# Attention scores in plain float32, two heads side by side, in a fused attention and two-layer-expert kernel

## Chip, cores and metric

One core of one Trainium2 chip. The time is device microseconds from start to end of one execution of the whole kernel; less is better. Engines: PE (TensorE matmul; PEld is its weight load), DVE (VectorE), ACT (ScalarE), POOL (GpSimd), SP (issues DMAs).

## What is computed

The reference is rotary attention, a gated layer (`x @ w_in`, times its sigmoid, `@ w_out`), and four relu experts weighted by `domain_probs`. The change touches the attention alone:

```python
batch, n_heads, seq, head_dim = (2, 8, 576, 64)
q_rot, k_rot = rotate(q), rotate(k)     # x1*cos - x2*sin, x1*sin + x2*cos
scores = q_rot @ k_rot.T / 8
attn = exp(scores - max(scores))
attn = attn / (sum(attn) + 1e-09)
out = attn @ v
```

All inputs and the output are float32.

## The kernel before

**Pairs and units.** The 16 heads are worked in 8 pairs of heads. Head 0 of a pair lies in partitions 0 to 63 of the tiles `xk` and `xq` (64 rows for the 64 head dimensions), head 1 in partitions 64 to 127. A pair has nine units: a unit (hf, r, h) is 128 query rows of head h against all 576 keys; r runs from 0 to 3, and the ninth unit (r = 4, h = 2) holds the last 64 query rows of both heads. Units 0 to 3 make half 0 of the pair, units 4 to 8 half 1.

**What a unit goes through.** `scores` (S below) multiplies query and key into a score tile `s` of two PSUM banks, 288 keys in each. `rowmax` (M, DVE) takes the negative row maximum. `expo` (E, ACT) makes the exponentials and their sums. `transp` (T, PE) transposes 4 x 128 columns into a PSUM bank `b`; `high` (H) copies that bank to SBUF on ACT, or, for the units listed in `EVD`, `low` (L) does it on DVE. The columns 512 to 575 of four units are transposed together into a further bank ("five" in the code, `p5`). `av` multiplies the transposed exponentials by the values in a bank, for half 1 of the pair before (`L0`, `L1`) and half 0 of this one (`P0`, `P1`); its result is copied to `xu` by ACT. `norm` (`Ln`, `Pn`) spreads the reciprocal sums into a bank by PE, and DVE multiplies `xu` by it (line 492), after which ACT and POOL split the product in two parts for the next layer.

**Keys and queries before.** Rotary is three operations for the key (k1 to k3) and three for the query (q1 to q3), on POOL or DVE (lines 252 to 259). The float32 key and query are then split in a high and a low float32r part: `key_high` on ACT, `key_low` on DVE, `query_high` and `query_low` on POOL (k4, k5, q4, q5), and `spread` sends six DMAs on SP's queue, so that a unit's stationary operand holds the high part of the query in 64 rows and the low part in the other 64, and the moving operand the keys twice. A unit's scores are four float32r matmuls of 128 rows and 288 columns (line 324), and ten matmuls for the ninth unit (lines 329 to 335). The first four units of the first pair alone go by `first_scores` (line 350): plain float32, 64 rows, one head, straight from `xq` and `xk`.

**PSUM.** Eight banks: two score tiles of two banks (`psS`), and four banks of the pool `ps1`, which the transposes, `p5`, `av` and `norm` take in turn.

**What sets the order.** The order of the instructions is written out by hand and kept (`manual_schedule`). Each unit is one step s = 0 to 8 of its pair, and the step's string in `ORDER` (`ORDER0` for the first pair, `ORDER2` for the last two) gives the order of atoms: S is the scores of unit i+2, M its row maximum, E the exponentials of unit i+1, T, H and L the transposes and copies of unit i, B the entries of `PLAN` (`av` and `norm`), v and V the copy and the multiply behind them, X the split, W and w the widening of the next layer's weights (`WIDE`). `OFF`, `OFF1`, `OFF2` place loads and rotary in half steps against the pair's start. Each engine works its own instructions strictly in this order.

**Behind the attention** come the gated layer and the experts, which nothing of the change touches; their first matmuls stand at the end of the last pair.

Of the kernel before, what the change touches and what calls it, by code (L numbers as in the profile page):

```python
# [38 lines left out]
NWARM = 13
NCST = 2 * 576 + 128 + 64 + 128  # L40
# [7 lines left out]
def fused_kernel(ctx, tc, q, k, v, w_in, w_out, dprobs, w1, w2, cst, out):  # L48
    nc = tc.nc
# [18 lines left out]
    mask = cs[:, 1344:1472]  # L68
    xh2 = pers.tile([128, 4, NT], F32R, name="xh")
# [145 lines left out]
    for p in range(NPAIR):  # L215
# [15 lines left out]
        if p == 0:  # L231
            P.units = [P.units[j] for j in FIRST]
# [28 lines left out]

    def parts(P, nm):
        t = kkp.tile([128, 2, 576], F32R, name=nm + "2")
        setattr(P, nm + "2", t)

    def key_high(P):
        for h in range(2):
            rows = (TOP, LOW)[h]
            nc.scalar.activation(KK[P.i][rows, 0, 576 * h:576 * h + 576], P.xk[rows, 0, :], AF.Copy,
                                 scale=0.125 if P.n > 1 else 1.0)  # L270

    def key_low(P):
        for h in range(2):
            rows = (TOP, LOW)[h]
            hi, lo = (KK[P.i][rows, z, 576 * h:576 * h + 576] for z in range(2))
            nc.vector.scalar_tensor_tensor(lo, P.xk[rows, 0, :], 0.125 if P.n > 1 else 1.0, f32(hi),
                                           ALU.mult, ALU.subtract)

    def spread(P):
        for h in range(2):  # L280
            k_ = f32(KK[P.i][:, :, 576 * h:576 * h + 576])
            nc.sync.dma_start(k_[(LOW, TOP)[h]], k_[(TOP, LOW)[h]])
            for z in range(2):
                nc.sync.dma_start(f32(QQ[P.i][64 * z:64 * z + 64, 640 * h:640 * h + 576]),
                                  f32(P.q2[64 * h:64 * h + 64, z, :]))
            made.add((P, "spread", h))

    def query_high(P, g, rows=ALL, cols=FULL):
        if g is nc.scalar:
            g.copy(P.q2[rows, 0, cols], P.xq[rows, 0, cols])  # L290
        else:
            g.tensor_scalar(P.q2[rows, 0, cols], P.xq[rows, 0, cols], 1.0, 1.0, ALU.mult, ALU.mult)

    def query_low(P, g, rows=ALL, cols=FULL):
        g.tensor_tensor(P.q2[rows, 1, cols], P.xq[rows, 0, cols], f32(P.q2)[rows, 0, cols], ALU.subtract)
# [4 lines left out]
    def prep_small(P):  # L300
# [4 lines left out]
        P.s = {}  # L305
# [4 lines left out]
    def scores(P, un):  # L310
        hf, r, h = un
        if P.n < 2 and P.units.index(un) < (NUN, NUN1)[P.n]:
            return first_scores(P, un)
        for h_ in (0, 1) if h == 2 else (h,):
            assert (P, "spread", h_) in made
        s = psS.tile([128, 2, 512], F32, name="s")
        kk, qq = KK[P.i], QQ[P.i]
        if r < 4:
            c0 = 704 if h else 0
            lq = qq[:, c0 + 128 * r:c0 + 128 * r + 128]  # L320
            for a in range(2):
                for nb in range(2):
                    c = 576 * h + 288 * nb
                    nc.tensor.matmul(s[:, nb, 0:288], lq, kk[:, a, c:c + 288],  # L324
                                     start=(a == 0), stop=(a == 1))
        else:
            for a in range(2):
                for nb in range(2):
                    nc.tensor.matmul(s[:, nb, 0:288], qq[:, 512:640], kk[:, a, 288 * nb:288 * nb + 288],
                                     start=(a == 0), stop=False)  # L330
            lq = qq[:, 576:704]
            for a in range(2):
                nc.tensor.matmul(s[:, 0, 0:288], lq, kk[:, a, 640:928], start=False, stop=(a == 1))
# [907 lines left out]
```

## Time and profile before

| | |
|---|---|
| median of 3 runs | 748.18 us (748.15 to 749.2) |
| the profiled execution's own time | 749.54 us |
| span of its records, first to last instruction | 746.8 us |
| PE busy by the records | 735.7 us (99%) |
| DVE, ACT, POOL busy | 484.8, 301.5, 267.1 us |
| mean granted TensorE clock | 0.988 |

The profiled execution lies 1.4 us above the median, and 2.7 us of its time lie outside its span. Matmul records overlap (a record lasts from the issue of its first column to the end of its results), so a busy PE says little by itself; what a matmul costs is read from the distance between the starts of neighbouring records. A plain float32 matmul leaves two records, a float32r matmul or a transpose one. PEclk 1.00 is 2.4 GHz, 0.50 is 1.2 GHz. The mark `[0.23 <-PE b L298]` behind a row says that the engine stood idle for 0.23 us and which instruction ended that.

### The profile page before, as it was taken

What the parts mean: (1) busy time and instruction counts of PE and PEld (TensorE: products, weight loads), DVE (VectorE), ACT (ScalarE), POOL (GpSimd) and SP (SyncE); (2) the same over time, 40 slices, a digit from 0 to 9 for tenths busy, and PEclk for the clock granted to TensorE, in tenths of its full rate; (3) what the DMA queues carried; (4) which work ended last, traced back from release to release, by engine and by line L of the source; (5) the groups of instructions that cost most, each with busy time, mean ns of one, the idle gap of its engine ahead of it and who ended that gap; (6) DMA issues with size and microseconds to landing.
All of it is one profiled execution on the core that took longest, in us unless ns stands there. A gap on an engine that the chain in (4) does not pass through costs nothing.

```text
span 746.8 us, 11306 instructions
## 1 busy us (share of the span) xinstructions
PE 735.7 (99%) x4398; PEld 663.5 (89%) x4398; DVE 484.8 (65%) x895; ACT 301.5 (40%) x671; POOL 267.1 (36%) x256
## 2 busy tenths in 40 slices
PE   7899999999999999999999999999999999999997
PEld 6677777779999999999998988989889899898996
DVE  6789889659999897974574544545445454454542
ACT  3577777555436144253241422413324133241320
POOL 3778888210004012035403516125161351613500
PEclk7899999999999999999999999999999999999999
DMA  7865663602331221331010301103011030110002
GB/s 229 239 189 145 173 173 82 195 1 58 108 116 59 81 90 57 114 113 47 13 56 0 113 1 57 57 1 113 0 57 58 1 113 1 57 58 0 1 29 99
DMA packets 25606, 58.91 MB, mean 79 GB/s; under 512 B 3280, under 2 KB 5328, under 8 KB 25552
## 3 DMA queue, kind: packets, MB, share of 16 engines
q1 hardware_dynamic: 23408, 57.42, 24.7%
q10 hardware_dynamic: 2144, 0.77, 0.4%
q8 instruction: 34, 0.56, 0.3%
q14 instruction: 20, 0.16, 0.1%
HBM read 46.39 MB, written 2.36 MB: 65 GB/s over the span
## 4 chain that ended last, share of the span: by engine, by line
PE 93%; DVE 2%; POOL 2%; issue 1%; DMA 1%; ACT 1%; SPq 0%; POOLq 0%; ACTq 0%; DVEq 0%
PE m L766 9%; PE m L767 9%; PE m L768 9%; PE m L695 7%; PE m L694 7%; PE m L693 7%; PE m L577 5%; PE m L579 5%; PE m L578 5%; PE m L601 4%; PE m L600 4%; PE m L602 4%; PE b L441 4%; PE b L298 4%; PE s L324 4%; PE b L444 1%
## 5 line engine op out<-in xcount | busy, mean ns | idle before, releaser
L772 DVE SCALAR_TENSOR_TENSOR acc<-m,dp,acc 128x512 f32<-128x512 f32 (+1 forms) x64 | 47.5, 742 | 108.1 <-PE m L768 108.1
L767 PE MATMUL m<-wl,gh 128*128 128x512 f32 (+1 forms) x292 | 113.1, 387 | 0.0
L766 PE MATMUL m<-wh,gh 128*128 128x512 f32 (+1 forms) x292 | 113.0, 387 | 0.0
L768 PE MATMUL m<-wh,gl 128*128 128x512 f32 (+1 forms) x292 | 112.7, 386 | 0.0
L714 DVE SCALAR_TENSOR_TENSOR gl<-g,gh 128x288 fp32r<-128x288 f32 x84 | 50.7, 603 | 45.0 <-ACT gh L713 43.2
L676 POOL TENSOR_TENSOR wl<-raw,wh 128x512 fp32r<-128x512 f32 x21 | 27.2, 1298 | 141.8 <-ACT wh L673 141.8
L589 POOL TENSOR_TENSOR gl<-g,gh 128x384 fp32r<-128x384 f32 x24 | 26.9, 1121 | 142.7 <-ACT gh L588 142.6
L357 DVE TENSOR_REDUCE nm<-s 128x1 f32<-128x576 f32 x72 | 53.6, 750 | 20.5 <-PE s L335 8.9
L695 PE MATMUL m<-xh,wl 128*128 128x288 f32 x224 | 66.1, 295 | 0.0
L694 PE MATMUL m<-xl,wh 128*128 128x288 f32 x224 | 66.0, 294 | 0.0
L693 PE MATMUL m<-xh,wh 128*128 128x288 f32 x224 | 65.9, 294 | 0.0
L367 ACT ACTIVATE p<-s,nm 128x576 f32<-128x576 f32 x72 | 53.5, 743 | 30.7 <-DVE nm L357 30.4
L768 PEld LDWEIGHTS m<-wh,gl 128*128 128x128 f32 x292 | 54.9, 188 | 11.4
L766 PEld LDWEIGHTS m<-wh,gh 128*128 128x128 f32 x292 | 54.8, 188 | 10.6
L600 PE MATMUL m<-gh,wh 128*128 128x384 f32 x192 | 64.1, 334 | 0.0
L601 PE MATMUL m<-gh,wl 128*128 128x384 f32 x192 | 64.1, 334 | 0.0
L602 PE MATMUL m<-gl,wh 128*128 128x384 f32 x192 | 64.1, 334 | 0.0
L767 PEld LDWEIGHTS m<-wl,gh 128*128 128x128 f32 x292 | 54.8, 188 | 10.3
L676 POOL TENSOR_TENSOR wl<-cvt,wh 128x512 fp32r<-128x512 f32 x28 | 36.2, 1294 | 69.7 <-ACT wh L673 69.7
L673 ACT CAST wh<-cvt 128x512 fp32r<-128x512 f32 x28 | 17.4, 623 | 89.3 <-DVE cvt L672 89.3
L324 PE MATMUL s<-kk,qq 128*128 128x288 f32 x240 | 48.6, 326 | 2.1 <-DMA qq<-q 1.8
L298 PE MATMUL b<-cs,p 128*128 128x128 f32 x320 | 48.7, 286 | 1.6 <-ACT p L367 1.5
(141 smaller groups left out, 1890.3 us busy)
## 6 DMA issues: line engine op xcount, KB each, us to landing
raw<-in_moe_w_dram SPq DMA_DIRECT2D x16, 1024.0 KB, 5.2
raw<-in_moe_w_out_dram SPq DMA_DIRECT2D x8, 1024.0 KB, 4.8
raw<-in_moe_w_in_dram SPq DMA_DIRECT2D x6, 1024.0 KB, 5.0
kk<-kk SPq DMA_DIRECT2D x16, 288.0 KB, 3.2
qq<-q SPq DMA_DIRECT2D x32, 144.0 KB, 3.3
xk<-in_k_dram SPq DMA_DIRECT2D x7, 576.0 KB, 5.8
xq<-in_q_dram SPq DMA_DIRECT2D x7, 576.0 KB, 6.8
xv<-in_v_dram SPq DMA_DIRECT2D x8, 320.0 KB, 6.0
```

The costliest lines, as they stand in the source:

```text
L298: nc.tensor.matmul(o, lhsT, idn[:, 0:n], is_transpose=True, start=True, stop=True)
L324: nc.tensor.matmul(s[:, nb, 0:288], lq, kk[:, a, c:c + 288], start=(a == 0), stop=(a == 1))
L600: nc.tensor.matmul(o, wh[:, f, ds], gh[:, cols], start=(f == 0), stop=False)
L601: nc.tensor.matmul(o, wl[:, f, ds], gh[:, cols], start=False, stop=False)
L602: nc.tensor.matmul(o, wh[:, f, ds], gl[:, cols], start=False, stop=(f == FT - 1))
L676: nc.gpsimd.tensor_tensor(lo, src(name), f32(hi), ALU.subtract)
L693: nc.tensor.matmul(ps, wh[:, k, ms], hh[:, k, cols], start=(first and k == 0), stop=False, skip_group_check=not first)
L694: nc.tensor.matmul(ps, wh[:, k, ms], hl[:, k, cols], start=False, stop=False, skip_group_check=not first)
L695: nc.tensor.matmul(ps, wl[:, k, ms], hh[:, k, cols], start=False, stop=(k == 1), skip_group_check=not first)
L766: nc.tensor.matmul(ps, gh[:, ts], wh[:, f, ds], start=(f == 0), stop=False)
L767: nc.tensor.matmul(ps, gh[:, ts], wl[:, f, ds], start=False, stop=False)
L768: nc.tensor.matmul(ps, gl[:, ts], wh[:, f, ds], start=False, stop=(f == FT - 1))
```

## The change

All scores are made as `first_scores` made them, straight from `xq` and `xk` in plain float32, and for both heads of a pair in one step: for each half of the keys the matmul of head 0 (rows 0 to 63) is followed by that of head 1 (rows 64 to 127), each into its own score tile. The ninth unit's two heads become 64-row, 64-column matmuls into partitions 0 to 63 and 64 to 127 of one tile. S therefore stands only in the steps before a unit with h = 0 (and the ninth), and M takes both heads' maxima. `key_high`, `key_low`, `query_high`, `query_low`, `spread` and their tiles go. The factor 1/8 of the later pairs' keys moves into a second pair of tables (`CT8`, `ST8`), loaded once at the start.

There are three score tiles (six banks), so that two banks are left: one for the transposes (`t`), one for everything else (`b`). Four of the five copies that DVE did for `EVD` go to ACT. The "five" of units 4 to 7 moves from step 7 to step 8. Of the rotary operations of pairs 2 to 7, k1, k3 and q3 go from POOL to DVE. The `av` of half 1 stands wholly in steps 0 and 1, and all orders and offsets are new.

```diff
-PLAN = [['L0'], ['L1'], [], ['Ln'], ['P0'], [], [], ['P1', 'Pn'], []]
+PLAN = [['L0', 'L1'], ['L2'], ['Ln'], [], ['P0'], ['P1'], ['P2'], ['Pn'], []]
+PLAN0 = [[], [], [], [], ['P0'], ['P1'], ['P2'], ['Pn'], []]
+PLAN2 = [['L0', 'L1'], ['L2'], ['Ln'], [], ['P0'], [], ['P1', 'P2'], ['Pn'], []]
-ORDER = ['ESTvVwBWXHLM', 'SBXTHEwvWVML', 'VSvXMTEwBHWL', 'BSTEvWVXMHLw', 'TESHBwVMWvXL', 'VSMvTEXWHwBL', 'VTvBSEMHwWLX', 'VSTMHvWwBLEX', 'WXSMTEHVLvwB']
+ORDER = ['ESTBHMLXwVvW', 'SEMBvXLTHVwW', 'STMEHLBvwXVW', 'LSTBMEWHVwvX', 'SETXHMLWVvwB', 'ESTMHvLBXWwV', 'TSBHLEMVwXvW', 'ESLTHMBXvVWw', 'ESTMBHWvLwVX']
+ORDER0 = ['ESTHMBVLXWwv', 'TESHLBMvVXWw', 'ELSTHMvVwWBX', 'SEMTHLVBXvWw', 'ESTHMBLXWvwV', 'ESMTHLWBVXvw', 'ETSBHLVMvXwW', 'SETHLMBvwXVW', 'ETSMBHLvXWwV']
+ORDER2 = ['SETHLvMBXVWw', 'ESMBTHvLXVwW', 'ESTBHLXMvVWw', 'ESTHMLvBWXVw', 'STEHLXBMwWvV', 'TSEMHBvLVXWw', 'STEMHLBWvXwV', 'SETHLMBXvVWw', 'SEMTHLvBXwVW']
-DV1 = ['q3', 'k2', 'q2']
-DVR = []
-EVD = [1, 3, 8, 4, 7]
+DV1 = ['q2', 'q1']
+DVR = ['k3', 'k1', 'q3']
+EVD = [6]
-DV0 = ['qb']
+DV0 = ['qc']
...
-    ps1 = actx.enter_context(tc.tile_pool(name="ps1", bufs=4, space=bass.MemoryType.PSUM, side="right"))
-    psS = ectx.enter_context(tc.tile_pool(name="psS", bufs=2, space=bass.MemoryType.PSUM))
+    ps1 = actx.enter_context(tc.tile_pool(name="ps1", bufs=1, space=bass.MemoryType.PSUM, side="right"))
+    psT = actx.enter_context(tc.tile_pool(name="psT", bufs=1, space=bass.MemoryType.PSUM, side="right"))
+    psS = ectx.enter_context(tc.tile_pool(name="psS", bufs=3, space=bass.MemoryType.PSUM))
...
         for nb in nbs:
-            nc.tensor.matmul(s[:, nb, 0:288], P.xq[rows, 0, c0:c0 + 128],
-                             P.xk[rows, 0, 288 * nb:288 * nb + 288], start=True, stop=True)
+            for h in range(2):
+                rows = slice(64 * h, 64 * h + 64)
+                x, y = P.xk[rows, 0, :], P.xq[rows, 0, :]
+                if r < 4:
+                    c0 = 128 * r + 64 * h
+                    nc.tensor.matmul(P.s[us[h]][:, nb, 0:288], y[:, c0:c0 + 128], x[:, 288 * nb:288 * nb + 288],
+                                     start=True, stop=True)
+                    continue
+                o, y = P.s[un][rows, nb, :], y[:, 0:64] if h else y[:, 512:576]
+                if h == 0:
+                    nc.tensor.matmul(o[:, 0:288], y, x[:, 288 * nb:288 * nb + 288], start=True, stop=True)
+                elif nb == 0:
+                    nc.tensor.matmul(o[:, 0:288], y, x[:, 64:352], start=True, stop=True)
+                else:
+                    nc.tensor.matmul(o[:, 0:224], y, x[:, 352:576], start=True, stop=True)
+                    nc.tensor.matmul(o[:, 224:288], y, x[:, 0:64], start=True, stop=True)
...
-        ps = bank(512)
+        ps = bank(512, "t", psT)
...
-        five = {(1, 1): (0, 1), (3, 1): (2, 3), (4, 2): (4,)}.get((r, h))
+        five = {(1, 1): (0, 1), (4, 2): (2, 3)}.get((r, h))
...
         def high():
-            if not late_copy:
-                nc.scalar.copy(dst, src)
-                if five:
-                    nc.scalar.copy(dst5, p5)
+            copy = nc.vector.tensor_copy if on_vector else nc.scalar.copy
+            copy(dst, src)
+            taken.remove("t")
+            if five:
+                copy(dst5, p5)
+                taken.remove("b")
...
-        return [(0.0, lambda j=j: mm(j)) for j in ((0, 1), (2, 3, 4))[part]]
+        return [(0.0, lambda j=j: mm(j)) for j in ((0, 1), (2, 3), (4,))[part]]
...
+        nc.sync.dma_start(cs[:, 1472:NCST], cst[:, 1472:NCST])
...
                 elif atom == "M":
-                    if i + 2 < len(allu):
+                    if i + 2 < len(allu) and allu[i + 2][1][2] != 1:
                         rowmax(*allu[i + 2])
+                        if allu[i + 2][1][2] == 0:
+                            rowmax(*allu[i + 3])
```

## Rows read from the trace of the kernel before

**Rows 1.** Page: the chain that ended last, share of the span by engine.
```profile
PE 93%; DVE 2%; POOL 2%; issue 1%; DMA 1%; ACT 1%; SPq 0%; POOLq 0%; ACTq 0%; DVEq 0%
```

**Rows 2.** Windows: stretch, its length, busy PE, PEld, DVE, ACT, POOL, PEclk, DMA, GB/s.
```profile
0.00:37.46 37.46, 30.53 (x148) 23.33 (x149) 25.55 (x44) 16.55 (x35) 20.53 (x26) 0.77 0.78 235
...
55.55:73.09 17.54, 17.39 (x129) 13.45 (x128) 16.94 (x28) 13.31 (x30) 14.97 (x14) 1.00 0.56 155
...
144.84:162.44 17.60, 17.56 (x127) 13.40 (x128) 12.38 (x27) 9.77 (x24) 2.88 (x6) 1.00 0.00 1
```

**Rows 3.** Timeline of PE in pair 2: start, length, line, tiles, form, count.
```profile
55.55 1.30 PE L441 MATMUL b<-pt,xv 128*64 128x320 f32 x8
56.77 0.80 PE L324 MATMUL s<-kk,qq 128*128 128x288 f32 x4
57.50 1.30 PE L441 MATMUL b<-pt,xv 128*64 128x320 f32 x8
58.72 0.81 PE L444 MATMUL b<-p,xv 128*128 128x320 f32 x2
59.37 0.60 PE L298 MATMUL b<-cs,p 128*128 128x128 f32 x4
59.72 0.78 PE L324 MATMUL s<-kk,qq 128*128 128x288 f32 x4
60.34 0.60 PE L298 MATMUL b<-cs,p 128*128 128x128 f32 x4
60.77 0.38 PE L298 MATMUL b<-cs,rb 128*128 128x128 f32 x2
...
61.13 0.78 PE L324 MATMUL s<-kk,qq 128*128 128x288 f32 x4
...
69.62 0.70 PE L444 MATMUL b<-p,xv 128*128 128x256 f32 x2
70.16 0.38 PE L298 MATMUL b<-cs,rb 128*128 128x128 f32 x2
```

**Rows 4.** Line 350 in three short windows: count, shortest/median/longest ns, first and last start.
```profile
L350 PE MATMUL s<-xk,xq x2: 402/454/507, 7.3 to 7.6; 64*128 64x288 f32 x2
...
L350 PE MATMUL s<-xk,xq x4: 684/765/846, 8.7 to 9.4; 64*128 64x288 f32 x4
...
L350 PE MATMUL s<-xk,xq x2: 684/684/684, 9.8 to 10.3; 64*128 64x288 f32 x2
```

**Rows 5.** Line 396 in a window of 0.08 us, same columns.
```profile
L396 PE MATMUL b<-cs,p x2: 267/267/267, 54.1 to 54.1; 64*64 64x64 f32 x2
```

**Rows 6.** Timeline: a wait of PE for ACT; a copy, a multiply, two row maxima.
```profile
35.98 0.19 ACT L367 ACTIVATION_READ_ACCUMULATOR p<-s,nm 128x1 f32 x1
36.23 0.79 PE L324 MATMUL s<-kk,qq 128*128 128x288 f32 x4 [0.30 <-ACT p L367]
...
60.97 0.59 ACT L405 COPY pt<-b 128x512 f32<-128x512 f32 x1 [0.23 <-PE b L298]
...
61.43 0.49 DVE L492 TENSOR_TENSOR xn<-xu,b 128x320 f32<-128x320 f32 x1
...
68.12 1.41 DVE L357 TENSOR_REDUCE nm<-s 128x1 f32<-128x576 f32 x2
```

**Rows 7.** First pair: windows with the clock (columns as in Rows 2), one timeline row.
```profile
20.00:25.00 5.00, 3.82 (x16) 3.43 (x17) 4.83 (x5) 2.20 (x4) 4.08 (x4) 0.50 0.76 264
...
25.00:26.00 1.00, 1.00 (x6) 0.68 (x5) 0.97 (x3) 0.00 (x0) 1.00 (x1) 0.74 0.93 194
...
21.18 1.30 PE L324 MATMUL s<-kk,qq 128*128 128x288 f32 x4 [1.83 <-DMA qq<-q]
```

**Rows 8.** Groups in 55.55 to 73.09: count, busy us, mean ns, idle before.
```profile
L411 DVE COPY pt<-b 128x512 f32<-128x512 f32 x5 | 3.4, 682 | 0.1
...
L276 DVE SCALAR_TENSOR_TENSOR kk<-xk,kk 64x576 fp32r<-64x576 f32 x2 | 1.8, 904 | 0.0
```

**Rows 9.** Page, DMA issues: count, size of one, median us from issue to landing.
```profile
xv<-in_v_dram SPq DMA_DIRECT2D x8, 320.0 KB, 6.0
```

More of the change, by code (lines that the diff above doesn't have):

```diff
@@ L254, in times @@
                 g.tensor_tensor(x[:, z, :], x[:, z, :], tab[rows, cols], ALU.mult)
+        scaled = nm == "k" and P.n > 1
         return [
-            lambda: times(0, CT),
-            lambda: times(1, ST),
+            lambda: times(0, CT8 if scaled else CT),
+            lambda: times(1, ST8 if scaled else ST),
             lambda: g.tensor_tensor(x[:, 0, :], x[:, 0, :], x[:, 1, :], ALU.add),
         ]
[L262 to L295, printed above, removed]
     def tr(o, lhsT, n=128):
@@ L304, in prep_small, with scores @@
         P.pt, P.xu, P.ps, P.rb = {}, {}, {}, {}
-        P.s = {}
+        P.s, P.turn = {}, [0, 0]
     def ucol(r, h):
         return 8 if r == 4 else 2 * r + h
-    def scores(P, un):
+    def scores(P, un, nbs=(0, 1)):
         hf, r, h = un
[L312 to L333, printed above, removed]
-                nc.tensor.matmul(s[:, 1, 0:256], lq, kk[:, a, 928:1184], start=False, stop=False)
-                nc.tensor.matmul(s[:, 1, 224:288], lq, kk[:, a, 576:640], start=False, stop=(a == 1))
-        P.s[un] = s
@@ L338, in first_scores @@
-    def first_scores(P, un, nbs=(0, 1)):
-        hf, r, h = un
-        if un not in P.s:
-            P.s[un] = psS.tile([128, 2, 512], F32, name="s")
-        s = P.s[un]
-        rows = slice(64 * h, 64 * h + 64)
-        c0 = 128 * r + 64 * h
-        need = {"ka", "qa"} | ({"kb"} if 1 in nbs else set()) | ({"qb"} if r else set()) | ({"qc"} if r > 1 else set())
-        if P.n:
-            need = {"k3", "q3"}
+        if h == 1:
+            return
+        us = [un] if r == 4 else [un, (hf, r, 1)]
@@ L348, in first_scores @@
+        if un not in P.s:
+            for x in us:
+                P.s[x] = psS.tile([128, 2, 512], F32, name="s")
+        need = {"k3", "q3"}
+        if not P.n:
+            need = {"ka", "qa"} | ({"kb"} if 1 in nbs else set()) | ({"qb"} if r else set()) | ({"qc"} if r > 1 else set())
         assert all((P, w) in made for w in need)
         for nb in nbs:
-            nc.tensor.matmul(s[:, nb, 0:288], P.xq[rows, 0, c0:c0 + 128],
-                             P.xk[rows, 0, 288 * nb:288 * nb + 288], start=True, stop=True)
+            for h in range(2):
[14 more added lines that the diff above has]
+                    nc.tensor.matmul(o[:, 224:288], y, x[:, 0:64], start=True, stop=True)
@@ L934, in attention @@
         P0.xq = yp.tile([128, 2, 576], F32, name="xq")
-        parts(P0, "q")
         nc.vector.memset(big[:], 2.0 ** 23)
@@ L989, in attention @@
             "qc": all_of(rotary(P0, "q", eng("qc"), ALL, QC)),
-            "h": lambda: key_high(P0), "l": lambda: key_low(P0), "sp": lambda: spread(P0),
-            "gh": lambda: query_high(P0, g), "gl": lambda: query_low(P0, eng("gl")),
-            "s0": lambda: first_scores(*allu[0], (0,)), "s1": lambda: first_scores(*allu[0], (1,)),
-            "s2": lambda: scores(*allu[1]),
+            "s0": lambda: scores(*allu[0], (0,)), "s1": lambda: scores(*allu[0], (1,)),
             "m0": lambda: rowmax(*allu[0]), "m1": lambda: rowmax(*allu[1]),
@@ L1008, in prepare @@
                     its[a] = lambda nm=nm, j=j, e=nc.vector if a in dve else g: rotary(Z, nm, e)[j]()
-            its["k4"] = lambda: key_high(Z)
-            its["k5"] = lambda: key_low(Z)
-            its["q4"] = lambda: (parts(Z, "q"), query_high(Z, g))
-            its["q5"] = lambda: (query_low(Z, nc.vector if "q5" in dve else g))
-            its["sp"] = lambda: spread(Z)
             its["lv"] = lambda: load_v(Z)
             at = {1: OFF1, 2: {a: n - 36 for a, n in OFF2.items()}}.get(Z.n, OFF)
-            for a in ("lk", "lq", "lv", "k1", "k2", "k3", "k4", "k5", "q1", "q2", "q3", "q4", "q5", "sp"):
+            for a in ("lk", "lq", "lv", "k1", "k2", "k3", "q1", "q2", "q3"):
                 if a in its:
@@ L1026, in attention @@
             prepare(Z)
[L1027 removed]
+        need = ["lk<k1", "lk<k2", "k1<k3", "k2<k3", "lq<q1", "lq<q2", "q1<q3", "q2<q3"]
         for Z in range(1, NPAIR):
@@ L1051, in background @@
                     if Z:
-                        items += norm(Z, hf) if what[1] == "n" else av(Z, hf, int(what[1]))
+                        items += norm(Z, hf) if what[1:] == "n" else av(Z, hf, int(what[1]))
                 run(items)
@@ L1125, in attention @@
         l1(0, 0, 0)
-        run(av(P, 1, 0))
-        run(av(P, 1, 1))
+        for part in range(3):
+            run(av(P, 1, part))
         evac()
```

82 lines of the change are left out of this document (36 added, 46 removed).

## The prediction, made before the changed kernel ran

> **What bounds the kernel now.** I read the page's chain first: PE makes 93% of what ended last [rows 1]. Then windows cut at the first `av` matmuls of each pair: before them lie 37.46 us with a busy PE of 30.5 and a mean clock of 0.77; the seven stretches from there to 162.44 last 17.54 to 18.37 us, 125.0 us in all or 17.85 each, with PE busy throughout and the clock at 1.00 [rows 2]. Behind 162.44 comes the part the change does not touch. So two things can move: the first 37 us, where PE waits and runs at half clock, and 7 x 17.85 us, where PE's own work is the limit. DVE's 16.94 of 17.54 us is close behind, ACT (13.3) and POOL (15.0) have room.
>
> **Price of a plain float32 score matmul.** At half clock its records begin 0.48 us apart (9.4, 9.8, 10.3). Where a matmul of each head is next in line, both run together: of the four records between 8.7 and 9.4, two last 846 and two 684 ns, one of each for either head, and they begin in twos [rows 4]. 0.48 us is two passes over 288 columns at 1.2 GHz, so a record is 0.24 us at 2.4 GHz, a matmul two records, and the second head is free. The first record of a group is 0.35 instead (7.3 to 7.6, full clock [rows 4]), because the second weights come late. Scores of two units: 0.35 + 3 x 0.24 = 1.07 us. Now one unit costs 0.62 (59.72 to 60.34), or 0.73 with a change of tile shape behind it (56.77 to 57.50) [rows 3]; two cost 1.24.
>
> **Price of a change of shape.** Eight 320-column `av` records in two 64-column strips need 4 x 0.267 us (two passes of 320 at 2.4 GHz) + 0.05 for weights = 1.12, yet the next group begins 1.22 later (55.55 to 56.77; 57.50 to 58.72) [rows 3]: 0.10 us where the tile shape changes. No row shows it at full clock for 64-row tiles. Bounds: 0 (groups of full 128-row tiles follow one another with none, 59.72 to 60.34 to 60.77 [rows 3]) and 0.14, half as much again as the nearest row. I take 0.10, the nearest. A pair has 10 such changes now (around four `av` groups and the ninth unit's small matmuls) and 17 afterwards.
>
> **The bank that holds the transposes.** Four transposes take 0.43 us (60.34 to 60.77); ACT begins the copy 0.63 after their start (60.97), needs 0.59, and PE goes on 0.06 after ACT has ended (36.17 to 36.23) [rows 3, 6]. With one bank `t`, two units' T stand at least 0.63 + 0.59 + 0.06 = 1.28 us apart. Now four banks hide that. In the bank `b`, "five" must wait until DVE has multiplied the spread sums out of it, and in the new orders DVE does two row maxima (1.41) ahead of that multiply (0.49 for 320 columns, 0.40 for 256) [rows 6].
>
> **A pair of the new kernel, step by step on PE** (c = 0.10):
> - From S of step 2: S 1.07 + c, T(2) at 1.17; its own next work would let T(3) start at 1.17 + 0.43 + Ln 0.36 = 1.96, the bank only at 2.45: wait 0.49. T(3) ends 2.88. Score results stand at 0.83 (last record) + 0.40 (its length [rows 4]) = 1.23; two maxima, multiply, hand-over 0.06: 3.19, so "five" waits 0.31; +0.22 + c = 3.51.
> - From S of step 4: T(4) 1.17; then 0.43, c, P0 (4 x 0.213 + 0.05 = 0.91), c: T(5) at 2.71; the same to T(6) at 4.25; 0.43, c, ninth unit's S 1.02, c, P2 0.54 (69.62 to 70.16 [rows 3]), c: 6.54. No wait.
> - From S of step 7: T(7) 1.17, Pn 0.22: free at 1.82, bank at 2.45: wait 0.63; ends 2.88; "five" waits for the multiply (1.23 + 1.41 + 0.40 + 0.06 = 3.10): 0.22; +0.22, c, small matmuls 0.16, c = 3.68.
> - From S of step 0: T(0) 1.17; 0.43, c, L0 and L1 8 x 0.267 + 0.05 = 2.19, c, fifth `av` matmul 0.65 (58.72 to 59.37 [rows 3]), T(1) 0.43, c = 5.17.
>
> Sum 18.90 us: 17.25 of work (a little under the 17.54 of the pair in [rows 2], four rounds of scores save 4 x 0.17, the ninth unit a little more, and seven more changes of shape take 0.7) and 1.65 of waits. Pairs 1 to 5: 5 x (18.90 - 17.85) = +5.25. Pair 6 has P1 and P2 together, two changes less: +0.85. The last pair has no next scores: about +0.7. **Together +6.8 us.** With c for the 64-row changes (8 of them) at 0 it is +1.2; at 0.14, +9.
>
> **What goes elsewhere costs nothing while PE sets the pace.** `key_low` (1.8) and four of five copies (2.7 of 3.4) leave DVE [rows 8]; three rotary operations come, of the 576 columns for which a row maximum takes 0.7: 16.94 [rows 2] becomes 14.5 at most. ACT takes 4 x 0.59 [rows 6] and loses `key_high`: 15.7 at most. POOL only loses. None reaches 18.9. `spread`'s six DMAs a pair leave SP's queue; the new table's DMA stands behind the first loads, and its first reader is pair 2's k1 in step 3. The values' load stands 5.5 steps later, in the step of its first reader (P0). SP runs ahead of the other engines, and holds it only behind the next loads of keys, whose third buffer is free after step 6 of the pair before; 6.0 us to landing [rows 9] end in step 1 or 2. Were either cover gone, PE would wait as long as the load is late.
>
> **The first pair.** Now PE waits 1.83 us for the spread's DMA alone, and the clock is 0.50 in 20 to 25 and up for half of the next us (0.74) [rows 7]. Afterwards no parts are waited for. By hand at half clock (S 0.64 + 3 x 0.48 = 2.08, T 0.85): first maxima at 10.1 as now, exponentials of unit 0 at 10.9; S of units 2, 3 needs unit 0's tile, 11.85; T(0) 14.1, T(1) 15.9 (after the copy), S, T(2) 19.1, T(3) 20.9, S, T(4) 24.5, clock up at 25.5 as now, T(5) 26.5, T(6) 28.1, T(7) 31.5, T(8) 32.8, S of the next pair 34.0, first `av` of pair 1 at 35.7 against 37.46: **-1.75 us**. Bounds: clock up at 18.6, 4.9 earlier than now; clock up a stretch later (28.8), nothing.
>
> **Sum.** +6.8 - 1.75 = +5.05 on the profiled 749.54, 754.6; on the median of the runs, 1.4 lower, 748.18 + 5.05 = **753.2 us**.
>
> **Rivals.**
> - *The bank waits do not come* (the engines drift so that T's copy is early). Then a pair takes 17.25: 7 x -0.6 - 1.75 = -6.0, **742.2**. For: PE is so full that waits of ACT and DVE are hidden now [rows 2]; against: the 1.28 us follow from one bank alone. It decides at under 0.6 us of PE's waits a pair. Faster.
> - *The clock comes up early.* Full rows of both heads side by side could do, in the first pair, what only 128-row work did: now PE was at half clock through nearly all its work on 64-row tiles (9.4 to 10.3 [rows 4], records 0.48 apart). At 18.6 instead of 25.5: T(8) at 29.7, -4.9 instead of -1.75, **750.1**; near no change if c is small too.
> - *The clock stays at half* through the first pair: of the 8.5 us between 25.5 and 34.0 PE's work would double, in part inside waits that are there anyway; I estimate +4: **757**.
> - *Unit 8's two heads do not run side by side.* They write one PSUM bank from two row strips. The row says they do: both 64 x 64 matmuls of line 396, also one bank, begin at 54.1 and last 267 ns [rows 5], with 64 columns only. Then 4 x 0.24 us more a pair: +7.7, **760.9**. The Trainium skill (TensorEngine Tiling (Array Packing), Gotcha 1: PSUM Pressure) says that different row tiles cannot access the same PSUM bank at once, which speaks against this change; by that rule the time would be the 760.9, and the trace does not agree with it.
> - *Two heads' full tiles do not overlap at full clock* either: excluded for half clock by [rows 4], and I give it nothing.
>
> **How the numbers follow.** Forecast 0.50; no bank waits 0.22; early clock 0.15; half clock 0.06; one bank 0.07. What a measurement can tell from no change is 0.2%, 1.5 us. Faster: 0.22, near half of the early clock, and 0.05 of the forecast's low end (c near 0): 0.34. Same: 0.05 of the early clock and 0.06 of the forecast: 0.11. Slower 0.55. The range reaches from just above the first rival's 742.2 to just below the last one's 760.9: 743 to 760; the forecast's own is 747 (c = 0, -1.75, less drift) to 757.
>
> **What would show it.** Right: stretches of some 18.9 us between first `av` matmuls; PE idle before T(3), T(8) ended by the ACT copy of `pt`, and before "five" ended by DVE `xn`, together 1.6 us a pair; score records of two heads starting together 0.24 apart; DVE at most 14.5 a pair; the first `av` of pair 1 at 35.7, PEclk 0.50 to 25. Wrong: a pair under 17.9, a clock that is back before 20, or an idle of PE that ACT's exponentials or POOL's rotary end.

## The result, and the profile after

The changed kernel takes **755.66 us** (median of 4 runs, 753.91 to 756.44) against 748.69 us (748.15 to 749.27) for the kernel before in the same session: a ratio of 1.009, 95% interval 1.0068 to 1.0112. It is 7.0 us slower; the forecast was 5.05 us slower. The profiled execution took 756.27 us with a span of 754.4 us, 7.6 us more than the 746.8 us of before (the two executions' own times differ by 6.7 us, because 1.9 us instead of 2.7 lie outside the span).

First the page of the changed kernel: the engines' busy time, the chain, and the group of all transposes with the idle time of PE ahead of them (the columns of before's page).

```profile
PE 739.6 (98%) x4398; PEld 644.1 (85%) x4398; DVE 456.3 (60%) x841; ACT 311.7 (41%) x703; POOL 216.8 (29%) x218
...
PE 96%; ACT 1%; DMA 1%; DVE 0%; issue 0%; SPq 0%; DVEq 0%; ACTq 0%
...
L262 PE MATMUL t<-cs,p 128*128 128x128 f32 x288 | 48.6, 293 | 7.3 <-ACT pt L358 7.3
```

DVE is busy 28.5 us less and POOL 50.3 us less, net of what was moved to DVE, ACT 10.2 us more, and PE's share of the chain rises from 93% [rows 1] to 96%. The last line is new: PE waits 7.3 us for the copy of `pt` out of the one bank `t`. Now the stretches, as in [rows 2], cut again at the first `av` matmuls of a pair:

```profile
0.00:36.25 36.25, 30.40 (x152) 19.34 (x152) 18.81 (x38) 15.70 (x36) 10.53 (x17) 0.76 0.52 188
36.25:55.42 19.17, 18.43 (x129) 11.28 (x129) 13.82 (x24) 15.30 (x35) 4.79 (x7) 1.00 0.32 106
...
36.25:170.31 134.06, 128.47 (x889) 79.58 (x889) 84.91 (x150) 99.85 (x236) 42.56 (x53) 1.00 0.23 82
```

This splits the 7.6 us. Up to pair 1's first `av` the kernel gains 37.46 - 36.25 = 1.2 us. The seven stretches take 134.06 us against 124.98 (37.46 to 162.44 in [rows 2]): 9.1 us more, 19.15 against 17.85 each. What follows, 754.4 - 170.31 = 584.1 us, is 0.3 us shorter than before. DVE is busy 13.82 us of pair 1's stretch (13.83 in pair 2, where before it was 16.94 [rows 2]), ACT 15.30, POOL 4.79, and PE still has the least room. So the loss lies in PE's own order. Here is PE in pair 1, from S of step 2 to S of step 2 of the next pair (timeline: start, length, line, tiles, form, count):

```profile
39.20 0.60 PE L262 MATMUL t<-cs,p 128*128 128x128 f32 x4
39.73 1.24 PE L292 MATMUL s<-xk,xq 64*128 64x288 f32 x8
40.90 0.66 PE L262 MATMUL t<-cs,p 128*128 128x128 f32 x4
...
41.61 0.33 PE L432 MATMUL b<-cs,rb 128*128 128x64 f32 x2
42.23 0.66 PE L262 MATMUL t<-cs,p 128*128 128x128 f32 x4 [0.29 <-ACT pt L358]
42.87 0.44 PE L262 MATMUL b<-cs,p 128*128 128x128 f32 x2
43.24 1.24 PE L292 MATMUL s<-xk,xq 64*128 64x288 f32 x8
...
48.20 0.45 PE L297 MATMUL s<-xk,xq 64*64 64x288 f32 x1
48.21 0.45 PE L299 MATMUL s<-xk,xq 64*64 64x288 f32 x1
...
49.95 1.24 PE L292 MATMUL s<-xk,xq 64*128 64x288 f32 x8
51.13 0.66 PE L262 MATMUL t<-cs,p 128*128 128x128 f32 x4
51.62 0.38 PE L262 MATMUL b<-cs,rb 128*128 128x128 f32 x2
52.46 0.66 PE L262 MATMUL t<-cs,p 128*128 128x128 f32 x4 [0.46 <-ACT pt L358]
53.03 0.44 PE L262 MATMUL b<-cs,p 128*128 128x128 f32 x2
...
53.66 1.24 PE L292 MATMUL s<-xk,xq 64*128 64x288 f32 x8
...
58.90 1.24 PE L292 MATMUL s<-xk,xq 64*128 64x288 f32 x8
```

Read it by starts. S, two units' scores, takes 40.90 - 39.73 = 1.17 us with the change of shape behind it, to the hundredth the 1.07 + 0.10 of the forecast. The spread of `rb` leaves PE free at some 41.75 (0.14 behind the start of its last part, as in [rows 3], 60.99 to 61.13), yet T(3) begins at 42.23, 0.48 us later: the mark names the ACT copy of `pt`. The same stands before T(8): the spread is done 0.22 behind 51.62, at 51.84, and T(8) begins 0.62 us later. Four transposes last 0.60 behind full-tile work (39.20) but 0.66 behind another tile shape or behind a wait (40.90, 42.23): that 0.06 matters below. Between them ACT and DVE do this (the timeline of the same kernel, the other engines):

```profile
41.00 1.42 DVE L308 TENSOR_REDUCE nm<-s 128x1 f32<-128x576 f32 x2 [2.51 <-PE s L292]
...
41.59 0.59 ACT L358 COPY pt<-t 128x512 f32<-128x512 f32 x1 [0.44 <-PE t L262]
...
42.34 0.47 DVE L446 TENSOR_TENSOR xn<-xu,b 128x320 f32<-128x320 f32 x1
```

T(2) at 40.90, copy at 41.59, 0.59 long, T(3) 0.05 after its end: 1.33 us from one T to the next through a single bank. And the multiply that frees `b` begins at 42.34 only, behind two maxima; "five" follows it at 42.87.

### The profile page after: what moved, and what is told of

Same layout as the page of the kernel before. It is cut to its first block, busy times and chain, and to the rows that moved or that the text cites. A ratio compares the mean times of both kernels' runs of the same rounds, so it can differ in the third digit from the quotient of the medians.

```text
span 754.4 us, 11092 instructions
## 1 busy us (share of the span) xinstructions
PE 739.6 (98%) x4398; PEld 644.1 (85%) x4398; DVE 456.3 (60%) x841; ACT 311.7 (41%) x703; POOL 216.8 (29%) x218
## 4 chain that ended last, share of the span: by engine, by line
PE 96%; ACT 1%; DMA 1%; DVE 0%; issue 0%; SPq 0%; DVEq 0%; ACTq 0%
PE m L721 9%; PE m L722 9%; PE m L723 9%; PE m L650 7%; PE m L648 7%; PE m L649 7%; PE t L262 6%; PE s L292 5%; PE m L532 5%; PE m L534 4%; PE m L533 4%; PE b L394 4%; PE m L556 4%; PE m L555 4%; PE m L557 4%; PE b L397 1%
## 5 line engine op out<-in xcount | busy, mean ns | idle before, releaser
L308 DVE TENSOR_REDUCE nm<-s 128x1 f32<-128x576 f32 x72 | 51.6, 753 | 48.3 <-PE s L292 44.0
L262 PEld LDWEIGHTS t<-cs,p 128*128 128x128 f32 x288 | 32.0, 145 | 30.9 <-ACT pt L358 16.7
L262 PE MATMUL t<-cs,p 128*128 128x128 f32 x288 | 48.6, 293 | 7.3 <-ACT pt L358 7.3
```

The costliest lines, as they stand in the source:

```text
L262: nc.tensor.matmul(o, lhsT, idn[:, 0:n], is_transpose=True, start=True, stop=True)
```

## The experiments

Eleven kernels, each the changed kernel with one edit, unless said otherwise. Ratios are against the kernel before, run in the same session. "A pair" is the distance between first `av` matmuls in the middle of the kernel; in the changed kernel it repeats within 0.02 us from pair 1 to pair 6 (pair 4 apart, 19.41, where one S comes late), so it tells more than the total, which also holds the first pair (see the clock, below).

**1. The other bank for T(3) and T(8).**

```diff
-        ps = bank(512, "t", psT)
+        swap = at == 3 or (at == 8 and P.n < NPAIR - 1)
+        ps = bank(512) if swap else bank(512, "t", psT)
+        bank5 = (lambda n: bank(n, "t", psT)) if swap else bank
```

> The transposes T(3) and T(8) take bank b and their two 'five' groups bank t; for this the spread of the reciprocals (Ln, Pn) moves ahead of T(2) and T(0), with its multiply ahead of the row maxima. Theory (a single bank for the transposes makes PE wait): the waits of PE for the ACT copy of pt before T(3) and T(8), 0.50 and 0.62 us a pair in the changed kernel, go, and so do the 0.15 + 0.15 us before 'five'; some of it may come back ahead of the moved spread. I expect 0.35 to 0.55 us less in each of the 7 pairs, 2.5 to 4 us, so 751.7 to 753.2 where the changed kernel has 755.7. Rival (ACT's pace, not the bank, sets these waits: whatever PE does next, it waits for ACT): no change, within 0.5 us.

Measured: 755.89 us (754.18 to 756.75), ratio 1.0091 (1.0075 to 1.0108), and a pair went from 19.17 to 19.45 us. PE's timeline in that kernel shows where the wait went:

```profile
57.57 0.60 PE L262 MATMUL b<-cs,p 128*128 128x128 f32 x4
58.41 0.44 PE L262 MATMUL t<-cs,p 128*128 128x128 f32 x2 [0.24 <-ACT pt L361]
58.78 1.60 PE L292 MATMUL s<-xk,xq 64*128 64x288 f32 x8
...
61.56 0.44 PE L397 MATMUL b<-pt,xv 128*64 128x256 f32 x2 [0.20 <-DVE xn L449]
```

T(3) (57.57) no longer waits, as the theory said. But "five" now waits for `t` (58.41), S takes 1.52 instead of 1.17 (58.78 to 60.30; its second head starts 0.36 us behind the first, when ACT has just ended the exponentials of the tile), and `av` waits for DVE's multiply (61.56). Neither side was right: the bank did cause the wait, and freeing it only passed the wait on, with 0.28 us on top. The edit also moves the spread and its multiply ahead, so that it does not tell the two moves apart.

**2. The multiply between the two maxima.**

```diff
-                        if allu[i + 2][1][2] == 0:
-                            rowmax(*allu[i + 3])
+                elif atom == "m":
+                    if i + 2 < len(allu) and allu[i + 2][1][2] == 0:
+                        rowmax(*allu[i + 3])
```

In the orders, m stands right behind M, but in the steps with Pn or Ln behind V.

> The two row maxima of a step are issued apart: in steps 2 and 7 the multiply that frees bank b stands between them, not behind both. Theory (what is left of PE's wait before 'five' is the queue on DVE: two maxima, then the multiply): the 0.15 + 0.15 us a pair go, 7 x 0.3 = 2 us at most, so 753.6 to 755; the second maximum comes 0.4 to 0.5 us later, which no score or transpose waits for. Rival (the wait before 'five' is hidden or moves elsewhere, as the second maximum delays the exponentials): no change or up to 1 us more.

Measured: 751.37 us (750.73 to 755.71, 10 runs), ratio 1.0044 (1.0028 to 1.006). The seven stretches:

```profile
33.39:165.38 131.99, 126.40 (x889) 79.80 (x888) 85.20 (x150) 99.24 (x236) 43.48 (x52) 1.00 0.24 83
```

A pair is 18.82 us, 0.35 less, and the seven stretches 2.07 us less, the theory's size. "Five" now follows T(3) (58.19 in PE's timeline) without a wait:

```profile
58.68 0.38 PE L262 MATMUL b<-cs,p 128*128 128x128 f32 x2
```

So the queue on DVE ahead of the multiply is shown as the cause of that wait. More than the waiting goes (0.15 and 0.08 us a pair by starts): the two transposes also last 0.38 instead of the 0.44 that they take behind a wait. The rest of the 4.3 us between the medians lies in the first pair (first `av` at 33.39, not 36.25), which is mostly the clock's: in this profile it is at 0.98 from 20 to 25 (experiment 6).

**3. The heads in turn.**

```diff
-        for nb in nbs:
-            for h in range(2):
+        for h in range(2):
+            for nb in nbs:
```

> Same matmuls, but both key halves of head 0 first and then both of head 1, so that neighbours in the queue use the same 64 rows of PE and only the last of one head and the first of the other can run together. Theory (the price 1.07 us for two units' scores rests on two heads running at once, at full clock too): of eight records of 0.24 us the number that have to follow one another rises from four to six or eight, 0.48 to 0.96 us more for each of 5 score groups of a pair: 2.4 us a pair at the low end, 17 us in 7 pairs, less where it falls in waits, so 767 to 790. Rival (the heads did not overlap, or PE takes the matmuls as it likes): no change.

Measured: 755.88 us, 1.0092 (1.0073 to 1.0112), a pair 19.19 us. One S in its timeline:

```profile
41.01 1.25 PE L292 MATMUL s<-xk,xq 64*128 64x288 f32 x8
42.19 0.33 PE L262 MATMUL t<-cs,p 128*128 128x128 f32 x1
```

From start to start 1.18 us, as with the heads alternating. No change: the theory's number fell, and two readings were left. Either PE runs the two heads together whatever their order, or they never ran together. Experiment 4 tells.

**4. Both heads in the same 64 rows.**

```diff
-                rows = slice(64 * h, 64 * h + 64)
+                rows = slice(0, 64) if r < 4 else slice(64 * h, 64 * h + 64)
```

> The scores of head 1 are taken from the 64 rows of head 0 (the ninth unit's stay as they are), so that the second half of the output's heads is computed from the wrong keys and queries; the number, the shapes and the order of the matmuls are those of the changed kernel, but both heads' matmuls sit in the same 64 rows of PE. Theory (two heads run side by side whatever their order in the queue, which is why issuing them in turn cost nothing): now they cannot, eight records of 0.24 us follow one another instead of four pairs, 4 x 0.24 = 0.96 us more for each of 4 score groups, 3.8 us a pair, about 23 in a pair, 27 us and more in all, 780 to 787. Rival (the heads never overlapped, the records only look so): no change, 755.

Measured: 786.2 us, ratio 1.0497 (1.0476 to 1.0517), a pair 22.68 us. One S in its timeline:

```profile
69.51 2.20 PE L292 MATMUL s<-xk,xq 64*128 64x288 f32 x8
71.64 0.33 PE L262 MATMUL t<-cs,p 128*128 128x128 f32 x1
```

S takes 71.64 - 69.51 = 2.13 us instead of 1.17: 0.96 more, which is 4 x 0.24. Two heads in different rows do run side by side at full clock and the second is free; in one strip they follow one another. The order in the queue does not matter (experiment 3), the rows do. Of 4 x 0.96 = 3.84 us a pair 3.51 arrived; that the rest filled waits is likely but not shown. The seven stretches make 22.6 of the 30.5 us; another 7.1 lie in the first pair, which ended at 43.35 instead of 36.25, with the granted clock at 0.50 until past 30.

**5. Two more changes of tile shape.**

```diff
-PLAN = [['L0', 'L1'], ['L2'], ['Ln'], [], ['P0'], ['P1'], ['P2'], ['Pn'], []]
+PLAN = [['L0'], ['L1', 'L2'], ['Ln'], [], ['P0'], ['P1'], ['P2'], ['Pn'], []]
...
-'SEMBvXLTHVwW'
+'SETHMBvXLVwW'
```

> The eight 64-column av matmuls of half 1 are taken apart: four behind T(0), four behind T(1) with the fifth, so that PE changes its tile shape twice more in a pair (19 changes instead of 17) and does the same work otherwise; T(0) and T(1) stay 1.6 us apart, more than the 1.28 that one bank needs. Theory (a change of shape costs 0.10 us, and the first transpose behind one 0.055 more): +0.2 to 0.3 us a pair, 1.4 to 2.2 us slower, 757.1 to 757.9. Rival (a change of shape costs nothing by itself; the time is in the matmuls): no change, within 0.5 us.

Measured: 755.69 us (755.48 to 759.0), 1.0101 (1.0084 to 1.0117). A pair is 19.47 us in every one of the stretches but the last, +0.30, and the seven are 1.84 us longer. PE's timeline:

```profile
53.16 1.30 PE L394 MATMUL b<-pt,xv 128*64 128x320 f32 x8
54.38 0.66 PE L262 MATMUL t<-cs,p 128*128 128x128 f32 x4
54.97 1.30 PE L394 MATMUL b<-pt,xv 128*64 128x320 f32 x8
56.20 0.81 PE L397 MATMUL b<-p,xv 128*128 128x320 f32 x2
56.93 0.51 PE L292 MATMUL s<-xk,xq 64*128 64x288 f32 x2
```

From the first `av` to the next S: 56.93 - 53.16 = 3.77 us, against 55.42 to 58.90 = 3.48 in the changed kernel, for the same matmuls. T(1) has become one of 0.66. The 0.29 us are not two changes alone. The fifth `av` matmul takes 0.73 to the next start with a change behind it, 0.65 without one [rows 3]: 0.08. T(1), which had a change behind it already, takes 0.59 instead of 0.53. The eight records in two groups take 1.22 and 1.23, in one group 3.48 - 0.65 - 0.53 = 2.30: 0.15 more, for a second change and a second start of a group (0.05 in the prediction). So the change itself costs 0.08 to 0.10 as forecast, and 0.15 on average with what hangs on it. The total missed its 757.1 to 757.9: the median hardly moved, because the profiled execution, and by their mean clock most of the others, had the clock back early (next).

**6. More work ahead of the first scores.**

```diff
-NWARM = 13
+NWARM = 22
```

> 22 instead of 13 dummy matmuls stand ahead of the first scores, which fill more of PE's idle time before the clock falls at 8.0 us. Theory (the first pair is paced by loads, DVE and ACT at first, and the clock comes back at some 25 us whatever is done before 8): within 1 us of the changed kernel, 755.7, the granted clock again 0.50 to about 25. Rival (the early clock of the prediction: PE kept busy up to the scores keeps its clock, or gets it back by 18.6): 3 to 4.4 us faster, 751.3 to 752.7.

Measured: 755.62 us (755.03 to 755.92), 1.009 (1.0077 to 1.0103). In its profiled execution the clock fell at about 11 instead of 8.0, yet came back at the same time (windows, columns of [rows 2]):

```profile
8.00:11.00 3.00, 1.70 (x9) 0.76 (x10) 2.08 (x5) 0.00 (x0) 1.40 (x3) 1.00 1.03 409
11.00:25.00 14.00, 12.12 (x44) 7.12 (x43) 7.75 (x15) 7.11 (x17) 3.59 (x3) 0.52 0.35 140
25.00:26.00 1.00, 1.00 (x10) 0.69 (x10) 1.00 (x2) 0.44 (x1) 0.00 (x0) 0.96 0.00 0
```

The theory holds for this edit. But the kernel of experiment 5, whose first pair is the changed kernel's own, instruction for instruction, had this in its profiled execution:

```profile
8.00:9.50 1.50, 0.55 (x6) 0.30 (x4) 0.98 (x3) 0.00 (x0) 0.68 (x2) 1.00 1.02 404
9.50:19.50 10.00, 8.88 (x31) 4.76 (x27) 5.75 (x10) 4.19 (x10) 3.46 (x4) 0.50 0.64 258
...
20.00:33.69 13.69, 12.56 (x91) 7.84 (x91) 8.79 (x17) 10.02 (x24) 5.81 (x6) 1.00 0.36 115
```

The clock is back before 20, and pair 1's first `av` stands at 33.69 instead of 36.25. The early clock of the prediction is thus real, worth 2.6 us, and comes without an edit to the first pair. The same goes for the later fall: here it is at 9.5, and in the profile of experiment 11, with 13 dummy matmuls, at about 11. That the added matmuls put it off is not shown. The changed kernel's four runs bear the mark: mean clock 0.989, 0.989, 0.991, 0.993 with 756.44, 756.27, 755.06, 753.91 us.

**7. Rotary back on POOL.**

```diff
-DVR = ['k3', 'k1', 'q3']
+DVR = []
```

> The rotary operations k1, k3 and q3 of pairs 2 to 7 go back from DVE to POOL. Theory (PE sets the pace, DVE and POOL both have room): no change, within 1 us; DVE's busy time in a pair falls by some 2 to 3 us, POOL's rises. If DVE's queue is behind PE's waits before 'five' and before the transposes, 1 to 2 us faster. Rival (POOL is too slow and the keys come late to the first scores of a pair): several us slower.

Measured: 756.69 us (754.18 to 757.43), 1.0096 (1.0076 to 1.0117). A quiet pair is 19.17 us as in the changed kernel, with DVE at 10.85 and POOL at 11.20 us of it (pair 2). Pairs 4 and 5 take 19.77 and 19.49 us, 0.36 and 0.32 more than in the changed kernel; in pair 5 a wait of 0.21 us of PE ends with POOL's `rb`. So where the rotary runs costs nothing in a quiet pair; the seven stretches were 0.7 us longer with it on POOL.

**8. Two score tiles, two banks each for `t` and `b`.**

```diff
-name="ps1", bufs=1,
-name="psT", bufs=1,
-name="psS", bufs=3,
+name="ps1", bufs=2,
+name="psT", bufs=2,
+name="psS", bufs=2,
```

> Undoes one part: two score tiles (four banks) as before, and two banks each for the transposes and for the rest; the orders stay. Theory: the waits for the banks go (1.4 us a pair less), but the scores of the next two units need both tiles, so S waits for the exponentials of the unit that is being transposed: by hand 1.2, 1.3, 1.5 and 1.6 us more before S of steps 0, 2, 4 and 7; together about +4 us a pair, 25 to 30 us slower, 780 to 786. Rival (the third tile was not needed, the bank waits are the whole loss): 7 x 1.4 = 10 us faster, 746.

Measured: 815.71 us (808.52 to 816.52), 1.0872 (1.0838 to 1.0907), a pair about 27.4 us: far over the 4 us a pair expected. Two views of pair 5, a window and the timeline of PE:

```profile
125.30:152.68 27.38, 22.41 (x130) 13.03 (x129) 14.38 (x25) 14.79 (x35) 7.09 (x9) 0.94 0.21 75
```

```profile
129.17 0.75 PE L292 MATMUL s<-xk,xq 64*128 64x288 f32 x2 [0.33 <-ACT p L318]
130.70 1.24 PE L292 MATMUL s<-xk,xq 64*128 64x288 f32 x6 [0.78 <-ACT p L318]
```

The transposes no longer wait, as expected: a second bank ends these waits. S does: one matmul goes when the first tile is free, and the other three 1.5 us later with the second, so that even the two heads' overlap is partly lost; and, with PE busy for only 22.41 of 27.38 us, the granted clock falls inside the pairs too (0.94 here). The theory named the right wait and left these two followers out. In these orders, which were made for three score tiles, the third is worth far more than the two banks that it takes; what two tiles would give in orders of their own was not tried (the kernel before has two, and 17.85 us a pair).

**9 to 11. Other work in the gaps.** If the loss is one missing bank and the changes of shape, the way back is to put work that needs neither bank where PE waits. In pairs 1 to 5 the order became S T(2) L2 T(3) Ln S "five" T(4), the ninth S, T(5) P0 P1 T(6) S T(7) P2 T(8) Pn S "five"; DVE copies `xu`; the maxima stay apart.

```diff
-PLAN = [['L0', 'L1'], ['L2'], ['Ln'], [], ['P0'], ['P1'], ['P2'], ['Pn'], []]
+PLAN = [['L0', 'L1'], [], ['L2'], ['Ln'], [], ['P0', 'P1'], [], ['P2'], ['Pn']]
...
+            fives.append(five_pe)
+            fivec.append(five_copy)
```

> Pairs 1 to 5 reordered so that other PE work stands where PE waited for the copy out of bank t: the fifth av matmul of half 1 between T(2) and T(3), that of half 0 between T(7) and T(8), the spread of the reciprocals behind T(3) and T(8), and the 'five' behind the next S; the copies of the av results go from ACT to DVE, and the maxima stay apart. The ninth unit's scores stand between T(4) and T(5), and the four av groups of half 0 together behind T(5): 2 changes of tile shape fewer in a pair. Theory (the loss is the single bank's waits plus the extra changes of shape): against the 18.82 us of a pair with the maxima apart, the wait before T(3) goes from 0.5 to 0.2, that before T(8) from 0.6 to 0.2, and 2 x 0.15 us of changes go: 17.7 to 18.1 us a pair, 3.6 to 5.6 us less in 5 pairs, 746 to 748, level with or just below the kernel before. Rival (the waits move on to the next hand-over, as when the banks were swapped, because ACT and DVE are the chain): 18.7 us a pair or more, 751 and above.

Measured: 754.27 us (751.8 to 754.99), 1.0065 (1.0051 to 1.0079); the pairs were uneven, 18.71 to 20.37 us. The rival was right. In the timeline T(8) waits again:

```profile
65.53 0.68 DVE L380 COPY pt<-t 128x512 f32<-128x512 f32 x1
...
66.13 2.07 DVE L308 TENSOR_REDUCE nm<-s 128x1 f32<-128x576 f32 x3
...
66.96 0.74 ACT L318 ACTIVATE p<-s,nm 128x576 f32<-128x576 f32 x1 [2.87 <-DVE nm L308]
...
67.70 0.58 ACT L380 COPY pt<-t 128x512 f32<-128x512 f32 x1
...
68.33 0.65 PE L262 MATMUL t<-cs,p 128*128 128x128 f32 x4 [0.93 <-ACT pt L380]
```

Read it upwards: T(8) waits for the copy of T(7), that stands on ACT behind the ninth unit's exponentials, those wait for its maximum, and that stands on DVE behind the copy of T(6). The ninth unit's scores had stood since 62.2, so its maximum could have come over 3 us earlier. It was moved:

```diff
-'EsTHBLWwX', 'TEHMmLWwX', 'ESLTHMmBvXWw'
+'EsnTHBLWwX', 'TEHeLWwX', 'SLTHMBvmXWw'
```

Here n is the ninth unit's maximum, e its exponentials.

> The kernel with the gaps filled, with what its trace showed to be late moved forward: the ninth unit's row maximum stands right behind its scores and its exponentials a step earlier (they held the copy of T(7) and so T(8) back by some 0.7 us a pair), q3 behind that maximum, the copy of the av result of half 0 between the two maxima of step 7, one widening step half a step later, and pair 6 has the same order. Theory: a pair takes the sum of PE's work, 17.4 to 17.5, and waits of 0.3 before T(3) and 0.2 before T(8): 18.0 us, at most 18.3; the seven stretches 126 to 128.5 us, 3 to 5.5 us less than with the maxima apart; 746 to 748.5, level with the kernel before (748.7) or just below. Rival (another hand-over of ACT or DVE is then late): 18.6 us a pair or more and 750 and above.

Measured: 751.42 us (750.06 to 753.63), 1.0041 (1.0025 to 1.0056); seven stretches of 130.8 us, the pairs 18.30 to 19.09. The rival was right again: in pairs 1 and 2 S waits 0.6 and 0.5 us for q3 on DVE, in pair 4 a T waits 0.8 us for a copy of `pt`. With q3 back on POOL and two steps of pair 4's widening later:

```diff
-DVR = ['k3', 'k1', 'q3']
+DVR = ['k3', 'k1']
...
-[33, 37, 37, 40, 42, 44, 45]
+[33, 38, 39, 40, 42, 44, 45]
```

> The last kernel (gaps filled, maximum of the ninth unit earlier) with the two late steps that its trace showed mended: q3 goes back to POOL, ahead of its other work (on DVE it ran 1.8 to 2 us beside POOL and held the first scores of a pair back by 0.5 us), and the widening of pair 4 a step later. Theory: six pairs of 18.2 to 18.3 us as pair 3 had, one of 18.6: 128 to 129 us for the seven stretches against 130.8, and 748.5 to 750 at the same clock, level with the kernel before within 0.2%. Rival (POOL's q3 is late): S of step 7 waits, 18.8 us a pair, 752 and above.

Measured: 751.67 us (748.94 to 752.4), 1.0028 (1.0015 to 1.0041).

```profile
35.63:165.45 129.82, 125.49 (x890) 79.61 (x889) 86.19 (x157) 95.59 (x224) 55.04 (x59) 1.00 0.24 85
54.09:72.38 18.29, 17.84 (x129) 11.25 (x129) 13.58 (x24) 13.83 (x32) 9.62 (x10) 1.00 0.31 112
```

The best pairs take 18.29 and 18.30 us, 0.88 less than the changed kernel's; 4.2 us of the 9.1 lost in the seven stretches came back. The theory had six pairs of 18.2 to 18.3; the other stretches took 18.45 to 18.60 and pair 4 19.18, where one S takes long. The total came out 1.7 us above its range, with the late clock in the profiled execution (first `av` at 35.63). These three kernels change several things at once, so their gains are not told apart. The kernel is 4 us faster than the change and still some 0.3% slower than the kernel before. Part of what is left is in PE's timeline:

```profile
68.35 0.60 PE L418 MATMUL b<-p,xv 128*128 128x256 f32 x2
69.19 0.66 PE L262 MATMUL t<-cs,p 128*128 128x128 f32 x4 [0.24 <-ACT pt L380]
```

With P2 between T(7) and T(8) the wait before T(8) fell from 0.62 to some 0.3 us (68.35 to 69.19 for work of 0.54, as in [rows 3]): the 1.33 us from T to T through one bank are not filled yet.

## Why the prediction was right, and where it was off

- **Direction and mechanism: right.** PE sets the pace on both sides of the change, none of its marked waits in the seven stretches ends with POOL or a DMA, and the single banks bring waits just before T(3), T(8) and "five": the first two end with ACT's copy of `pt` by their marks, the last 0.06 us behind DVE's multiply (42.34 + 0.47 to 42.87), and it goes when the multiply comes earlier (experiment 2). Of the prediction's four segments of a pair the trace shows 3.51 (39.73 to 43.24; forecast 3.51), 6.71 (43.24 to 49.95; 6.54), 3.71 (49.95 to 53.66; 3.68) and 5.24 (53.66 to 58.90; 5.17): 19.17 against 18.90.
- **The price of scores: right.** 1.17 us for S with its change of shape, measured as forecast; 64-row tiles do cost 0.10 at full clock (T(1) before S takes 39.73 - 39.20 = 0.53, of which 0.43 are its own). The prediction says that no row shows this, and bounds it by 0 and 0.14. The trace of before had a row for it, in pair 2, four transposes ahead of the small matmuls of the ninth unit:

```profile
70.91 0.60 PE L298 MATMUL b<-cs,p 128*128 128x128 f32 x4
71.44 0.33 PE L396 MATMUL b<-cs,p 64*64 64x64 f32 x4
```

That is 0.53 us from start to start, there too. With it the wide bounds, +1.2 to +9 us for the pairs, could have been drawn close around 0.10.
- **PE's work in a pair, "17.25 of work": mis-sized.** It is some 17.84, the 19.17 less the waits below. Nearly all of the missing 0.59 us is one detail: behind a change of shape or a wait, the four transposes take 0.66 instead of 0.60 [rows 3], the first of them lasting 0.164 to the next start instead of 0.109 by single records, and a pair has ten such groups, "five" included: 10 x 0.055 = 0.55. I had let a change cost the same 0.10 (at most 0.14) whatever came behind it. Why the first transpose takes longer is not shown. So PE's work in a pair is no shorter than the whole pair before (17.85 on average): the changes of shape have eaten what the scores save, and the waits are the loss.
- **The waits, "1.65": too high.** 0.48 + 0.62 before T(3) and T(8) by the timeline, and 0.15 and 0.08 before "five" (42.23 to 42.87 and 52.46 to 53.03, where four transposes of this kind take 0.49): 1.33 in all. Those before "five" came out smaller, in part because the transposes ahead of them took longer. This error and the one above run against each other, 0.59 and 0.32 us a pair; that the pair came out within 0.27 us is partly luck.
- **The first pair, "-1.75": 1.2 in the profiled execution**, with the clock back at 25 as forecast. In other executions, where it is back early, about 2.6 us more is gained. In the profile of experiment 1, whose first pair differs by one spread and two banks, it is back by 19 and the first `av` stands at 32.86, 4.6 us earlier than before's 37.46, near the 4.9 of the second rival. So that rival had the price about right, but the first pair that the change made had the clock early in some executions and late in others: its 0.15 was put on the wrong thing. No row of before gives its 18.6, nor the 28.8 of the other bound; among the profiles of kernels with about this first pair the clock came back between 19 (experiment 1) and 26 (experiment 3).
- **The sum.** -1.2 + 9.1 - 0.3 = +7.6 in the profiled execution, and +7.0 between the medians, against +5.05; of the 2.3 us by which the seven stretches exceed the forecast's +6.8, 1.9 is (19.17 - 18.90) x 7 and 0.24 one late S in pair 4.
- **The rivals.** No bank waits: they came. Half clock through the first pair: no. The ninth unit's heads one after the other: they begin at 48.20 and 48.21 in the timeline above, with 288 columns and one bank, and run together. By the rule of the Trainium skill (TensorEngine Tiling (Array Packing), Gotcha 1: PSUM Pressure) they could not; the trace does not agree with it.

## What to carry to other kernels

Where PE is the limit, a change that shortens its matmuls also changes what stands beside them: count the changes of tile shape (0.10 us each here, 0.15 where a group of transposes follows) and the banks that are left for hand-overs (1.33 us from one transpose group to the next through one bank) before counting the saving. A wait for a shared bank was not removed here by using another busy bank; it shrank when independent work was put into the gap, or when what frees the bank was moved ahead of unrelated work in its engine's queue. Total times that hold a warm-up at a varying clock hide effects of some 0.3%; compare the steady stretches.

## What the runs showed of the hardware that was not expected

- Two matmuls in different halves of PE's rows run together even if another matmul of the first half stands between them in the program: with the heads in turn S stayed at 1.18 us, in one strip it became 2.13.
- Two 64 x 64 tiles with 288 columns in different partitions of one PSUM bank start 0.01 us apart and run side by side.
- With the same instructions in the first pair, the granted clock fell to 0.50 at 8 us and came back at 25 in one profiled execution, and fell at 9.5 and came back before 20 in another.
